# Softcap attention and a bilinear FFN on one core: load order, PSUM banks, row buffers and the start addresses of tiles

## The chip, the cores and the metric

The kernel runs on one core of one Trainium2 chip. The metric is device time in microseconds. A core has five engines that run side by side and wait for one another by semaphores: TensorE (matmuls, PE in the profile), VectorE (DVE), ScalarE (ACT), GpSimd (POOL) and SyncE (SP, which here issues most DMAs). Each engine works off its own instructions in the order in which they were written.

## The reference

```python
def _attn_ref(q, k, v, cap):              # q, k, v: (4, 12, 448, 64) float32
    scores = np.matmul(q, k.transpose(0, 1, 3, 2)) / np.sqrt(q.shape[-1])
    scores = cap * np.tanh(scores / cap)
    scores = scores - np.max(scores, axis=-1, keepdims=True)
    attn = np.exp(scores)
    attn = attn / (np.sum(attn, axis=-1, keepdims=True) + 1e-09)
    return np.matmul(attn, v)

def _moe_ref(x, w_a, w_b, w_out):         # x: (1792, 768), w: float64, d_ff 1536
    return ((x @ w_a) * (x @ w_b) @ w_out).astype(np.float32)
```

x is the attention output with the heads side by side. The weights arrive as float64, two 32-bit words per value.

## The kernel before

**Attention.** 48 heads are taken two at a time: 24 pairs, `NPG` = 12 of them make a group, which is half of the tokens. For a pair, `load_k` loads q and k in four blocks of 32 columns each (56 KB, runs of 128 bytes), `load_v` loads v in four pieces, `turn` transposes q and k in 32x32 blocks on VectorE. `scores` multiplies them in four chunks of keys (c = 0, 1, 2 of 128 keys per head and c = 3 with the last 64 of both heads), each into a PSUM tile of two banks. `tanh` and `exp` run on ScalarE; the softmax needs no maximum, since the cap bounds the scores. `add_full` and `add_last` add the chunks up on VectorE, `sums` adds that over partitions with 28 small matmuls against the selector `sel`, and `attend` multiplies the exponentials with v into one PSUM bank, `pv`. `recip` inverts the sums, `store_rec` writes them to memory (`rd`), `load_den` reads them back as a row for 64 partitions each (`den`), `scale` multiplies pv with it.

The first group's matmuls are in fp32 (each is two instructions), and its x is split at once into a high and a low fp32r part (`split_x`: `xhi`, `xlo`). The second group's scores are in fp32r with three products of high and low parts; its x goes to memory and comes back later.

**FFN.** `hidden` makes 448 tokens by 128 columns of x @ w_a or x @ w_b in 18 fp32r matmuls of 448 columns, `project` makes 128 tokens by 384 columns of the output in 9 of 384 columns, each into one PSUM bank. `keep_a`, `gate` and `collect` empty the banks. A weight is loaded as float64 words (`load64`, 768 KB), converted in six steps (`conv`: two on ScalarE, three on VectorE, one on GpSimd) and split (`split_hi`, `split_lo`).

**Order.** The order on TensorE is written by hand in `chain`: for the first group the four score chunks of a pair, then attend and sums of the pair before; then FFN pieces of the first group between the attention of the second (`ffn(GAP / 2)` twice a pair), then the second group's FFN. A planner places everything else: each job has an engine, a duration, a lag and what it needs, gets a due time back from TensorE's order, and each engine takes the ready job with the earliest due time. The fourth `job` argument after the needs, `after`, is an earliest time in the plan. It only orders the plan; on the chip an instruction waits for its data and its buffers alone.

**Buffers.** A pool with a tag and `bufs` hands out that many buffers, and the first instruction on a buffer waits for the last reader of the tile that had it. [...] In the first group scores have three tiles of two banks (`sc_one`) and pv has two banks; later scores have two tiles, the FFN two and one (`ff_a`, `ff_b`), pv one. In SBUF the tiles stand one behind the other; the framework's constants end at a multiple of 128 bytes, `capt` and `bounded` take 64 bytes, then come `sel` (512 bytes a partition), `psum0`, `psum1`, `xhi`, `xlo`, `acc` and the rest, all multiples of 128.

Of the kernel before, what the change touches and what calls it, by code (L numbers as in the profile page):

```python
# [118 lines left out]
def kernel(  # L119
# [54 lines left out]
    ps = {}  # L174

    def psum_pool(name, bufs, instead=None):
        if instead is not None:
            ps.pop(instead).close()
        ps[name] = fast.enter_context(ExitStack())
        side = "right" if name[:2] == "pv" or name == "ff_b" else "left"  # L180
        pool = tc.tile_pool(name=name, bufs=bufs, side=side, space=bass.MemoryType.PSUM, reuse_waits="tile")
        return ps[name].enter_context(pool)

    room = {"pv": psum_pool("pv_one", 2), "sc": psum_pool("sc_one", 3)}
# [4 lines left out]
    sel = const.tile([P, SUB, Q], F32, tag="sel", name="sel")  # L189
# [8 lines left out]
    raw, stk, prob, pvs = {}, {}, {}, {}  # L198

# [12 lines left out]
    def load_v(pi, n):  # L212
# [3 lines left out]
        eng = nc.gpsimd if 2 <= pi < NPG else nc.sync  # L216
# [30 lines left out]
    def scores(pi, c):  # L247
        tk, tq = stk["k", pi], stk["q", pi]
        psc = room["sc"].tile([P, 2, 512], F32, tag="pssc", name=f"psc_{pi}_{c}")
# [16 lines left out]
    def tanh(pi, c):  # L266
        hf, i = divmod(c, 2)
        if i == 0:
# [21 lines left out]
    def attend(pi, hf):  # L290
        if hf == 0:
            pvs[pi] = room["pv"].tile([P, 512], F32, tag="pv", name=f"pv_{pi}")
# [6 lines left out]
    def sums(pi):  # L299
        t = pvs[pi]  # L300
        for m in range(SUB):
            for i in range(P // Q):
# [6 lines left out]
                nc.tensor.matmul(to, sel[:, m], psum[pi % 2][:, j, c * SC : (c + 1) * SC], start=(m == 0), stop=last)  # L309

    def recip(pi):
        rec = sm.tile([P, SC], F32, tag="rec", name=f"rec_{pi}", bufs=1)
# [12 lines left out]
    xs, hold = {}, {}  # L325

# [97 lines left out]
    FB0 = 6  # L424

    def bank(name):
        n = len(took)
        took.append(name)
        if n == 0:
            room["sc"] = psum_pool("sc_two", 2, "sc_one")  # L430
            room["ff", 0] = psum_pool("ff_a", 2)
        elif n == FB0:
            room["pv"] = psum_pool("pv_two", 1, "pv_one")
            room["ff", 1] = psum_pool("ff_b", 1)
        late = n >= FB0 and (n - FB0) % 3 == 0
        return room["ff", int(late)].tile([P, 512], F32, tag="ff", name=name)

    took = []

# [58 lines left out]
    class Piece:  # L498
        def __init__(self, eng, us, lag, needs, fn, args, after):
            self.eng, self.us, self.lag, self.needs, self.fn, self.args, self.after = eng, us, lag, needs, fn, args, after  # L500
            self.due, self.then, self.order_only = 1e9, [], False
# [7 lines left out]
    def loads(pi, after=0.0):  # L509
        for nm in "kq":  # L510
            eng = "ACT" if nm == "q" and pi == 0 else "SP"
            for n in range(P // BLK):
                needs = [("load", nm, pi, n - 1)] if n else [("turn", nm, pi - 2)]
                job(("load", nm, pi, n), eng, 0.52, load_k, (pi, nm, n), needs, 2.4, after)
                jobs["load", nm, pi, n].order_only = n > 0
        for n in range(4):
            eng, us = ("POOL", 0.6) if 2 <= pi < NPG else ("SP", 0.52)
# [4 lines left out]
    def softmax(pi):  # L522
        for c in range(SUB):
            needs = [("tanh", pi, c - 2)] if c > 1 else []
            if c % 2 == 0:
                needs += [("attend", pi - 2, c // 2), ("add", pi - 2, c // 2)]
            if c == 2:
# [8 lines left out]
        job(("recip", pi), "DVE", 0.5, recip, (pi,), [("sums", pi), ("rd", pi - 1)])  # L536
        job(("rd", pi), "SP", 0.5, store_rec, (pi,), [("recip", pi)])
        free = [("x", pi - 2)]
        for j in range(2):
            job(("den", pi, j), "SP", 0.52, load_den, (pi, j), [("rd", pi), *([("den", pi, 0)] if j else free)])  # L540
# [18 lines left out]
    chain = []  # L559
# [5 lines left out]
    def scores_of(pi, c):  # L565
        ready = [("lo", nm, pi) for nm in "kq"] + ([("z", pi)] if c == NC3 else []) if pi >= NPG else [("turn", nm, pi) for nm in "kq"]
        back = 3 if pi < NPG else 2
        n = SUB * pi + c - back
        if (NPG - 1) * SUB < n < NPG * SUB and pi >= NPG:
            n = NPG * SUB - 1  # L570
# [266 lines left out]
```

## Time and profile before

| | us |
|---|---|
| median of 3 runs (739.11 to 1163.57) | 741.04 |
| profiled execution | 739.0 |
| its span, first to last instruction | 737.1 |
| TensorE busy | 711.3 (96%) |
| VectorE, ScalarE, GpSimd busy | 438.6, 347.7, 107.1 |
| granted TensorE clock, mean | 0.988 |

The busy time of TensorE counts pipelined matmuls whose ends are modelled, so 96% doesn't say that it runs at its peak. How fast matmuls follow one another is read from their start times in the timeline. The slowest of the three runs is far off the other two; the profile is of an execution beside these.

### The profile page before, as it was taken

The numbers are of one execution on the slowest core, as the hardware profiler recorded it, in microseconds if no ns is written. First come the engines' busy times: TensorE is split into PE (matmuls) and PEld (weight loads), VectorE is DVE, ScalarE is ACT, GpSimd is POOL, SyncE is SP. The second block draws the span as 40 slices with busy tenths as digits, with TensorE's granted clock in tenths as the row PEclk, the third lists the DMA queues.
The fourth block names the chain that finished last, engine by engine and source line by source line (L and its number), as shares of the span: only waits on it lengthen the run. The fifth ranks groups of instructions, "written<-read, shape, count | busy, mean of one in ns | idle before, by whom it ended". The sixth has DMA issues, their size and how long they took to land.

```text
span 737.1 us, 10930 instructions
## 1 busy us (share of the span) xinstructions
PE 711.3 (96%) x4242; PEld 578.7 (79%) x4242; DVE 438.6 (60%) x657; ACT 347.7 (47%) x474; POOL 107.1 (15%) x86
## 2 busy tenths in 40 slices
PE   5987999999999999999999999999999999999996
PEld 2333337788887798778788779999999999999996
DVE  3588988968766877885986747442033434334222
ACT  3888785676875864675757630122321112202100
POOL 2224242222212312312222100000000000000000
PEclk8899999999999999999999999999999999999999
DMA  9679675656866665656355427322022103101012
GB/s 163 121 130 161 129 165 149 163 177 167 211 194 167 172 175 162 185 167 179 117 178 154 141 82 256 108 86 64 1 86 65 43 22 108 44 21 44 1 44 110
DMA packets 141914, 90.53 MB, mean 123 GB/s; under 512 B 107104, under 2 KB 127648, under 8 KB 141856
## 3 DMA queue, kind: packets, MB, share of 16 engines
q1 hardware_dynamic: 137152, 82.53, 42.4%
q0 software_dynamic: 2848, 7.02, 3.6%
q8 instruction: 35, 0.57, 0.3%
q10 hardware_dynamic: 1856, 0.23, 0.3%
q14 instruction: 23, 0.19, 0.1%
HBM read 67.24 MB, written 22.50 MB: 122 GB/s over the span
## 4 chain that ended last, share of the span: by engine, by line
PE 83%; DMA 7%; SPq 3%; DVE 3%; ACT 2%; issue 1%; POOL 0%; ACTq 0%; DVEq 0%; POOLq 0%
PE phb L445 8%; PE phb L447 8%; PE phb L446 8%; PE pha L445 8%; PE pha L446 8%; PE pha L447 8%; PE po L478 8%; PE po L480 7%; PE po L479 7%; PE pv L297 7%; PE psc L260 3%; DMA den<-rd 3%; SPq L210 2%; DMA rd<-rec 2%; PE psc L255 2%; PE psc L263 1%
## 5 line engine op out<-in xcount | busy, mean ns | idle before, releaser
L478 PE MATMUL po<-who,gh 128*128 128x384 f32 x336 | 113.4, 338 | 1.9 <-DVE acc L489 1.5
L480 PE MATMUL po<-who,gl 128*128 128x384 f32 x336 | 112.4, 334 | 0.0
L479 PE MATMUL po<-wlo,gh 128*128 128x384 f32 x336 | 112.3, 334 | 0.0
L445 PE MATMUL pha<-xhi,wha 128*128 128x448 f32 x288 | 106.1, 369 | 0.8 <-DVE xhi L345 0.8
L445 PE MATMUL phb<-xhi,whb 128*128 128x448 f32 x288 | 106.1, 369 | 0.0
L446 PE MATMUL pha<-xlo,wha 128*128 128x448 f32 x288 | 105.8, 367 | 0.2 <-DVE xlo L346 0.2
L447 PE MATMUL pha<-xhi,wla 128*128 128x448 f32 x288 | 105.7, 367 | 0.0
L447 PE MATMUL phb<-xhi,wlb 128*128 128x448 f32 x288 | 105.6, 367 | 0.0
L446 PE MATMUL phb<-xlo,whb 128*128 128x448 f32 x288 | 105.6, 367 | 0.0
L272 ACT ACTIVATE pf<-psc,capt 128x896 f32<-128x896 f32 x96 | 82.7, 912 | 35.3 <-PE psc L260 20.0
L297 PE MATMUL pv<-pf,vb 128*64 128x448 f32 x384 | 79.2, 555 | 6.4 <-DVE den L329 6.4
L276 ACT ACTIVATE pf<-pf,capt 128x1792 f32<-128x1792 f32 (+1 forms) x48 | 77.2, 1611 | 0.5
L489 DVE TENSOR_TENSOR acc<-po,acc 128x384 f32<-128x384 f32 x84 | 46.2, 554 | 41.5 <-PE po L480 41.4
L452 ACT COPY asb<-pha 128x448 f32<-128x448 f32 x48 | 25.6, 533 | 93.3 <-PE pha L447 91.3
L464 ACT CAST gh<-asb 128x448 fp32r<-128x448 f32 x48 | 27.2, 567 | 88.5 <-DVE asb L462 88.1
L297 PEld LDWEIGHTS pv<-pf,vb 128*64 128x64 f32 x384 | 25.8, 138 | 53.1 <-issue 39.2
L478 PEld LDWEIGHTS po<-who,gh 128*128 128x128 f32 x336 | 63.0, 188 | 4.8 <-DVE acc L489 2.7
L462 DVE TENSOR_TENSOR asb<-phb,asb 128x448 f32<-128x448 f32 x48 | 29.9, 622 | 59.7 <-PE phb L447 59.6
L479 PEld LDWEIGHTS po<-wlo,gh 128*128 128x128 f32 x336 | 63.1, 188 | 0.2
L480 PEld LDWEIGHTS po<-who,gl 128*128 128x128 f32 x336 | 63.1, 188 | 0.0
L445 PEld LDWEIGHTS pha<-xhi,wha 128*128 128x128 f32 x288 | 54.1, 188 | 6.9 <-DVE xhi L345 1.2
L445 PEld LDWEIGHTS phb<-xhi,whb 128*128 128x128 f32 x288 | 54.1, 188 | 6.3 <-issue 1.2
(94 smaller groups left out, 1049.2 us busy)
## 6 DMA issues: line engine op xcount, KB each, us to landing
w64o<-in_moe_w_out_dram SPq DMA_DIRECT2D x12, 768.0 KB
w64a<-in_moe_w_a_dram SPq DMA_DIRECT2D x9, 768.0 KB
w64b<-in_moe_w_b_dram SPq DMA_DIRECT2D x9, 768.0 KB
ldk<-in_k_dram SPq DMA_DIRECT2D x96, 56.0 KB
den<-rd SPq DMA_DIRECT2D x48, 112.0 KB
ldq<-in_q_dram SPq DMA_DIRECT2D x92, 56.0 KB
out_dram<-acc SPq DMA_DIRECT2D x13, 384.0 KB
wda<-wta SPq DMA_DIRECT2D x12, 384.0 KB
```

The costliest lines, as they stand in the source:

```text
L272: nc.scalar.activation(to, prob.pop((pi, "s", c))[:, :n, :S], AF.Tanh, scale=capt[:, 1:2])
L276: nc.scalar.activation(pf, pf, AF.Exp, scale=capt[:, 0:1])
L297: nc.tensor.matmul(t[o, :S], tv[:, j * (NC3 + 1) + (c if j == 0 else (c + 1) % (NC3 + 1))], p, start=(c == 0), stop=(c == NC3))
L445: nc.tensor.matmul(t[:, :S], wh[:, kk], xhi[:, kk, cs], start=(kk == 0), stop=False)
L446: nc.tensor.matmul(t[:, :S], wh[:, kk], xlo[:, kk, cs], start=False, stop=False)
L447: nc.tensor.matmul(t[:, :S], wl[:, kk], xhi[:, kk, cs], start=False, stop=(kk == NK - 1))
L462: nc.vector.tensor_mul(t, phs.pop(("b", h))[:, :S], t)
L464: nc.scalar.copy(gs[g, f][0][:, cs], t)
L478: nc.tensor.matmul(t[:, :HALF], gh[:, cs], wh, start=(f == fs[0]), stop=False)
L479: nc.tensor.matmul(t[:, :HALF], gh[:, cs], wl, start=False, stop=False)
L480: nc.tensor.matmul(t[:, :HALF], gl[:, cs], wh, start=False, stop=(f == fs[-1]))
L489: nc.vector.tensor_add(acc[:, ti, hs], t, acc[:, ti, hs])
```

## The change

- Loads: v of pair 2 is loaded from SP and not from GpSimd; `cap` is loaded from ScalarE's queue behind q of pair 0; the planned earliest time of the weight loads goes from 12.0 to 18.0 (`RAW`); longer lags are planned for the first loads, for `rd` and for `den`. The warm-up is five matmuls (ten instructions) and comes ahead of the other memsets.
- PSUM: two score tiles throughout, and one pool of four single banks for pv and the FFN.
- Order on TensorE: in the first group chunks 0 and 1, attend of the pair before, chunks 3 and 2, sums of two pairs before. `GAP` 20.4; 3.6 us of FFN pieces around pair 12. A piece of `hidden` may be planned before its later x rows are there (`early`).
- The selector is a block of ones in a tile of 56 columns, from which a window is taken.
- `rec` has two buffers; `den` of pairs 10 and 11 is lent from the FFN's gate buffers.
- Addresses: `sel` moves to the end, a tile of 64 bytes, `even`, stands in its place.

```diff
-    room = {"pv": psum_pool("pv_one", 2), "sc": psum_pool("sc_one", 3)}
+    ps_sc = fast.enter_context(tc.tile_pool(name="ps_sc", bufs=2, space=bass.MemoryType.PSUM))
+    ps_1 = fast.enter_context(tc.tile_pool(name="ps_1", bufs=4, space=bass.MemoryType.PSUM))
+
+    def bank(name):
+        return ps_1.tile([P, 512], F32, tag="ps1", name=name)
...
-    sel = const.tile([P, SUB, Q], F32, tag="sel", name="sel")
+    const.tile([P, 16], F32, tag="even", name="even")
...
+    ends = fast.enter_context(tc.tile_pool(name="ends", bufs=1))
+    sel = ends.tile([P, 2 * Q - QS], F32, tag="sel", name="sel")
...
-        eng = nc.gpsimd if 2 <= pi < NPG else nc.sync
+        eng = nc.gpsimd if 3 <= pi < NPG else nc.sync
...
-                nc.tensor.matmul(to, sel[:, m], psum[pi % 2][:, j, c * SC : (c + 1) * SC], start=(m == 0), stop=last)
+                nc.tensor.matmul(to, sel[:, Q - (m + 1) * QS : 2 * Q - (m + 1) * QS], psum[pi % 2][:, j, c * SC : (c + 1) * SC], start=(m == 0), stop=last)
...
-            pvs[pi] = (pvs[pi][0], sm.tile([P, S], F32, tag="den", name=f"den_{pi}"))
+            if pi in LENT:
+                den = f32(gp.tile([P, GT], F32R, tag=LENT[pi], name=f"den_{pi}", bufs=GF)[:, :S])
+            else:
+                den = sm.tile([P, S], F32, tag="den", name=f"den_{pi}")
+            pvs[pi] = (pvs[pi][0], den)
...
+    LENT = {NPG - 2: "gh", NPG - 1: "gl"}
...
-                job(("load", nm, pi, n), eng, 0.52, load_k, (pi, nm, n), needs, 2.4, after)
+                job(("load", nm, pi, n), eng, 0.52, load_k, (pi, nm, n), needs, 3.2 if pi < 2 else 2.4, after)
...
-            on_pe(("attend", pi, hf), 1.52, attend, (pi, hf), [("exp", pi, hf), free, *(("load", "v", pi, n) for n in range(4))])
+            on_pe(("attend", pi, hf), 1.52, attend, (pi, hf), [("exp", pi, hf), *banks[-4:-3], *(("load", "v", pi, n) for n in range(4))])
+        banks.append(("scale", pi))
...
-    WARM, SOON = 3, 4.0
-    GAP = 19.4
+    WARM, SOON, RAW = 5, 4.0, 18.0
+    GAP = 20.4
...
-        for c in range(SUB):
+        for c in (0, 1):
             scores_of(pi, c)
         if pi:
             attend_of(pi - 1)
+        for c in (3, 2):
+            scores_of(pi, c)
+        if pi > 1:
+            sums_of(pi - 2)
...
-            job(("raw", t), "POOL" if t < 6 else "SP", 0.6, load64, (t,), [("conv", t - 2, 5)], 6.0, 12.0)
+            job(("raw", t), "POOL" if t < 6 else "SP", 0.6, load64, (t,), [("conv", t - 2, 5)], 6.0, RAW)
...
+        warm = bank("warm")
+        nc.vector.memset(psum[0][:, 0], 0.0)
+        for _ in range(WARM):
+            nc.tensor.matmul(warm[:, :S], psum[0][:, 0, :P], psum[0][:, 0], start=True, stop=True)
...
+    def load_cap():
+        nc.scalar.dma_start(capt[:, 3:4], cap.rearrange("(a b) -> a b", b=1).to_broadcast([P, 1]))
+
+    job("cap", "ACT", 0.5, load_cap, (), [("load", "q", 0, 3)], 2.4)
```

## Rows read from the trace of the kernel before

**Rows 1.** The page, busy time, its share of the span, and instructions.

```profile
PE 711.3 (96%) x4242; PEld 578.7 (79%) x4242; DVE 438.6 (60%) x657; ACT 347.7 (47%) x474; POOL 107.1 (15%) x86
```

**Rows 2.** Timeline, stretch 0 to 110: start us, length, engine, line, out<-in [idle <-releaser].

```profile
2.75 4.48 PE L710 MATMUL warm<-psum 128*128 128x448 f32 x6 [2.75 <-DVE psum L708]
...
3.97 0.86 POOL L365 DMA_DIRECT2D w64a<-in_moe_w_a_dram  x1
...
8.08 0.65 DVE L226 STREAM_TRANSPOSE tq<-ldq 128x448 f32<-128x448 f32 x1 [4.91 <-DMA ldq<-in_q_dram]
...
9.31 5.07 PE L255 MATMUL psc<-tq,tk 64*128 64x448 f32 x16 [2.08 <-DVE capt L718]
...
18.05 6.20 PE L255 MATMUL psc<-tq,tk 64*128 64x448 f32 x16 [3.68 <-DVE tq L226]
...
27.62 0.89 ACT L375 ACTIVATE w64a<-w64a 128x768 int32<-128x768 uint32 x1
...
27.92 3.43 PE L255 MATMUL psc<-tq,tk 64*128 64x448 f32 x16
...
109.71 0.47 PE L445 MATMUL pha<-xhi,wha 128*128 128x448 f32 x1
```

**Rows 3.** Busy time by stage: stretch, length, engines, granted clock, DMA share, GB/s.

```profile
27.90:59.70 31.80, 28.17 (x222) 10.79 (x216) 24.54 (x39) 28.38 (x28) 10.12 (x16) 1.00 0.76 127
59.70:79.50 19.80, 16.57 (x148) 6.48 (x149) 17.29 (x26) 14.94 (x15) 9.16 (x12) 0.91 0.85 169
79.50:109.70 30.20, 28.49 (x246) 11.27 (x240) 28.10 (x42) 27.13 (x27) 10.97 (x14) 1.00 0.71 149
```

**Rows 4.** Waits from 27.9 to 109.7: engine line <- releaser: us, times, longest.

```profile
PE pv L297 <- DVE den L329: 6.4, 4, 2.4
...
PE pv L309 <- DVE psum L283: 1.8, 2, 1.0
```

**Rows 5.** Groups of instructions by shape: busy us, mean ns | idle before.

```profile
L478 PE MATMUL po<-who,gh 128*128 128x384 f32 x336 | 113.4, 338 | 1.9 <-DVE acc L489 1.5 <-DVE asb L462 0.3
...
L445 PE MATMUL pha<-xhi,wha 128*128 128x448 f32 x288 | 106.1, 369 | 0.8 <-DVE xhi L345 0.8
...
L272 ACT ACTIVATE pf<-psc,capt 128x896 f32<-128x896 f32 x72 | 68.9, 1005 | 35.3 <-PE psc L260 20.0 <-PE psc L255 14.7 <-DVE rec L313 0.6
...
L479 PEld LDWEIGHTS po<-wlo,gh 128*128 128x128 f32 x336 | 63.1, 188 | 0.2
...
L309 PEld LDWEIGHTS pv<-psum,sel 128*32 128x32 f32 x672 | 11.7, 109 | 19.7 <-DVE psum L283 6.8 <-DVE gl L467 2.1 <-issue 2.1
```

**Rows 6.** Timeline of TensorE: first and last of 55 hidden, of 94 projection matmuls.

```profile
480.04 0.37 PE L445 MATMUL pha<-xhi,wha 128*128 128x448 f32 x1
...
491.20 0.37 PE L445 MATMUL phb<-xhi,whb 128*128 128x448 f32 x1
...
515.01 0.33 PE L478 MATMUL po<-who,gh 128*128 128x384 f32 x1
...
531.13 0.33 PE L478 MATMUL po<-who,gh 128*128 128x384 f32 x1
```

**Rows 7.** Timeline, weight loads of fp32 attend: first and last of six steps.

```profile
24.61 0.14 PEld L297 LDWEIGHTS pv<-pf,vb 128*64 128x64 f32 x2 [0.23 <-issue]
...
26.49 0.14 PEld L297 LDWEIGHTS pv<-pf,vb 128*64 128x64 f32 x2 [0.23 <-issue]
```

**Rows 8.** DMA issues by line and engine: KB each, median us from issue to landing.

```profile
w64a<-in_moe_w_a_dram POOLq DMA_DIRECT2D x3, 768.0 KB, 6.3
```

**Rows 9.** Chain that ended last, in order of time: start us, us, what.

```profile
14.89 2.42 DMA vb<-in_v_dram
...
147.73 1.43 PE psc L260 x12
```

**Rows 10.** Timeline of VectorE behind the last attend: reciprocal and scale.

```profile
441.65 0.56 DVE L313 RECIPROCAL rec<-pv 112x64 f32<-112x64 f32 x1 [1.60 <-PE pv L309]
...
451.71 0.62 DVE L329 TENSOR_TENSOR den<-pv,den 128x448 f32<-128x448 f32 x1 [1.74 <-DMA den<-rd]
```

More of the change, by code (lines that the diff above doesn't have):

```diff
@@ L422 @@
     phs, asb, gs = {}, {}, {}
[L424 to L438, printed above, removed]
     def hidden(g, f, nm, h):
@@ L523, in softmax @@
         for c in range(SUB):
[L524 to L527, printed above, removed]
+            needs = [("attend", pi - 2, c // 2), ("add", pi - 2, c // 2)]
+            if c > 1:
                 needs += [("add", pi - 2, "l")]
@@ L535, in softmax @@
         g, r = divmod(pi, NPG)
-        job(("recip", pi), "DVE", 0.5, recip, (pi,), [("sums", pi), ("rd", pi - 1)])
-        job(("rd", pi), "SP", 0.5, store_rec, (pi,), [("recip", pi)])
-        free = [("x", pi - 2)]
+        job(("recip", pi), "DVE", 0.5, recip, (pi,), [("sums", pi), ("rd", pi - 2)])
+        job(("rd", pi), "SP", 0.7, store_rec, (pi,), [("recip", pi)], 3.0)
+        own_den = [p for p in range(pi) if p not in LENT]
+        free = [("x", own_den[-2])] if pi not in LENT and len(own_den) > 1 else []
         for j in range(2):
-            job(("den", pi, j), "SP", 0.52, load_den, (pi, j), [("rd", pi), *([("den", pi, 0)] if j else free)])
+            job(("den", pi, j), "SP", 0.52, load_den, (pi, j), [("rd", pi), *([("den", pi, 0)] if j else free)], 3.0)
             jobs["den", pi, j].order_only = j > 0
@@ L593, in ffn_piece @@
             on_pe(key, 3.6, hidden, (g, f, x, h), needs)
+            kind = "xl" if g else "x"
+            jobs[key].early = {id(jobs[kind, h * NP + kk]): 0.6 * kk for kk in range(NP) if (kind, h * NP + kk) in jobs}
             if x == "a":
@@ L659 @@
                 scores_of(pi, c)
-            ffn(GAP / 2)
-            for c in range(2, SUB):
+            ffn(GAP / 2 if pi > NPG else 3.6)
+            for c in (3, 2):
                 scores_of(pi, c)
-            ffn(GAP / 2)
+            ffn(GAP / 2 if pi > NPG else 3.6)
     ffn(1e9)
@@ L702, in warm_up @@
     def warm_up():
[L703 to L710 removed]
+        warm = bank("warm")
+        nc.vector.memset(psum[0][:, 0], 0.0)
+        for _ in range(WARM):
+            nc.tensor.matmul(warm[:, :S], psum[0][:, 0, :P], psum[0][:, 0], start=True, stop=True)
+        for t in vb:
+            for j in range(2):
+                nc.vector.memset(t[own[1 - j], NC3 + j], 0.0)
         nc.vector.memset(sel, 0.0)
@@ L713, in warm_up @@
             nc.vector.memset(f32(z), 0.0)
-        for m in range(SUB):
-            nc.vector.memset(sel[:, m, m * QS : (m + 1) * QS], 1.0)
+        nc.vector.memset(sel[:, Q - QS : Q], 1.0)
     def limits():
@@ L786 @@
             y.left -= 1
-            y.ready = max(y.ready, t + x.us if y.order_only and y.eng == x.eng else x.end)
+            y.ready = max(y.ready, t + x.us if y.order_only and y.eng == x.eng else x.end - y.early.get(id(x), 0.0))
             if not y.left and y.eng != "PE":
@@ L794 @@
             x.fn(*x.args)
-    for pool in reversed(ps.values()):
-        pool.close()
     fast.close()
```

58 lines of the change are left out of this document (18 added, 40 removed).

## Prediction

> **What bounds the kernel now.** I read the page first: TensorE is busy in 96% of the span [rows 1], so a gain can only come from the few places where it waits, or from its matmuls following one another faster. The profiled execution took 739.0 us, 1.9 more than its span of 737.1, and the median of the runs shown is 741.0; I sum against 739.0.
>
> For the waits I read the timeline of the start. Scores begin at 9.31 for the first pair, 18.05 for the second and 27.92 for the third [rows 2]. The cause stands beside it: the first transpose waits 4.91 us for the last block of q, while a weight load of 768 KB, issued by GpSimd at 3.97 (a second one follows it), moves on the same DMA engines [rows 2]. Next I read the busy time by stage, from the third pair to the first FFN matmul at 109.71: TensorE is busy 28.17 + 16.57 + 28.49 = 73.2 of 81.8 us, ScalarE 70.5, VectorE 69.9 [rows 2, 3]. Three engines are near their limit, none at it. (The granted clock of the middle stage is 0.91: part of it ran at the lower level, 1.2 GHz; that stays in the 73.2.) The list of waits for that stretch tells where TensorE's 8.6 idle us go: 6.4 to attend waiting for the scale of two pairs back (store of the reciprocals, load of the rows, product), 1.8 to sums waiting for the adds [rows 4]. From 109.7 on TensorE hardly waits, apart from 0.8 us for xhi [rows 5].
>
> So the rest of the time is the pace of the FFN matmuls, and here the timeline shows something odd. Projection matmuls (384 columns) follow one another in (531.13 - 515.01) / 93 = 173.3 ns, hidden ones (448 columns) in (491.20 - 480.04) / 54 = 206.7 ns [rows 6]. At 2.4 GHz that is 416 and 496 columns, 32 and 48 more than they stream. It isn't a fixed cost of every matmul: the fp32 attend steps come each (26.49 - 24.61) / 5 = 376 ns for 448 columns passed twice, 373.3 + 2.7 [rows 7]. Nor is it the time of a weight load: 32 columns take 109 ns and 128 take 188 [rows 5], so 0.82 ns a column, 105 ns for 128, well under 160.
>
> **The change part by part.**
>
> *Alignment.* The two tiles ahead of `sel` take 64 bytes and all later sizes are multiples of 128, so before the change every operand starts 64 bytes past a multiple of 128; `even` in place of `sel` puts it on the multiple. If a moving operand is fetched in lines of 128 bytes (32 columns), 384 columns from the middle of a line touch 13 of them, and 13 x 32 = 416 is to the column what the row shows. 448 columns touch 15, 480 columns, and the row shows 16 more [rows 6]. Aligned, one line goes: 13.3 ns a matmul. There are 6 x 288 hidden and 3 x 336 projection matmuls [rows 5]: 2736 x 13.3 ns = 36.5 us. Bounds: nothing, if the excess has nothing to do with addresses; and all of it above the 2.7 ns that fp32 shows, 17.3 x 1728 + 10.6 x 1008 ns = 41 us. I take 36.5, because 13 lines fit without a remainder and because fp32, where a column has two clocks and an extra line has time to arrive, shows no such cost at the same offset.
>
> [...]
>
> *First loads.* The v loads of pair 2 leave GpSimd's queue, and the weight loads are planned from 18.0 on instead of 12.0. By the planner's own durations k and q of pair 0 are there at 4 x 0.52 + 3.2 = 5.3, its first tanh starts at 7.8, its second exp ends at 14.4 and its attend at about 17.3. That is below 18.0, so the v loads of pair 3 come first in GpSimd's queue; they wait for that attend to free their buffer, and the weight loads are queued behind this wait. What is late next is the conversion of the weights. It began at 27.62 [rows 2]; issued near 20, with 6.3 us to land [rows 8], the first weights come near 27, and TensorE needs them near 100: nothing. The 448 KB of the first q and k then have the DMA engines alone. cap goes behind q on ScalarE's queue, where only the table load and the first tanh are behind it, and leaves SP's head, 0.4 us. Ten warm-up instructions instead of six, 0.75 us each [rows 2], end at 7.5 to 8.8, about when the first scores can start; they hide under the loads. SP then issues 8 blocks for pair 1 at some 0.5 us (the planner's figure), 2.42 us to land [rows 9], 1.25 for two transposes: scores near 13. v of pairs 0 and 1 and q, k of pair 2 are 16 more issues: third scores near 20.5 instead of 27.92. v of pair 2 puts four issues, 2.1 us, on SP; the loads of pair 3 behind them have a pair's time of 7 us to spare.
>
> *Order of the fp32 phase, banks, selector, lent rows.* Sums move one pair later and attend gets four banks, so a scale has two more attends' time before anyone waits: the 6.4 and 1.8 us go. Against it, scores keep two buffers instead of three, and attend stands between chunks 0, 1 and 3, 2, so a chunk's tanh has to end while TensorE does other work. The trace has no such order. Bounds: nothing (two tanh take 2 us [rows 5], attend over 3), and one tanh of 1.0 us for each of ten pairs, 10 us. ScalarE and VectorE are busy 70 of the 73 us, so they follow with little slack, and I take 5.3 us. First FFN matmul: 20.5 + 73.2 + 5.3 = 99.0 against 109.7, 10.7 us gained, with ends of 1 and 18 (loads and waits both at their worst or best). The selector has as many matmuls of the same size: nothing. A second `rec` and two lent rows only take away waits of SP and VectorE that TensorE doesn't see: nothing.
>
> *FFN phase.* GAP and the new order move pieces between pairs; their number stays. The first pieces may start before all x are split: the 0.8 us goes. pv now shares four banks with the FFN instead of having its own; if the pool hands on the bank that was freed first, the FFN keeps three in turn, as before: nothing.
>
> Sum: 739.0 - 36.5 - 10.7 - 0.8 = 691.0 us.
>
> **Rivals.**
>
> *Addresses don't matter*; the excess belongs to one-pass matmuls, or to a weight swap that fp32's double pass hides. For it: every operand stands at the same offset, so no row compares two. Against it: the fit to 416. Then 739.0 - 11.5 = 727.5. [...] No run shows a second offset yet.
>
> *pv's bank stalls the FFN.* If banks go round strictly, the fourth piece behind an attend waits for its scale. From the reciprocal to the end of the scale it took 452.3 - 441.7 = 10.7 us [rows 10]; two score chunks and three projections take 1.43 [rows 9] + 3 x 1.56 = 6.1. In the new order four projections follow the attends of pairs 14, 17 and 20, and that of pair 23 without scores: 3 x 4.6 + 6.0 = 20 us, 711. Three hidden pieces take 11 us and hide it.
>
> *Aligned starts cost.* The 16 columns that the line count leaves over at 448 [rows 6] say that something else, such as how the weight stream and the moving stream meet, matters too; both starting on a line's edge could meet worse. From 11.5 us / 2736 = 4.2 ns more per matmul the kernel is slower than before; a line more, 13.3 ns, gives 764. Against it: nothing in a row makes an aligned start the worse one.
>
> **How the numbers follow.** Forecast, 691: 0.52. Addresses don't matter, 727: 0.27. Bank stalls, 711: 0.10. Aligned starts cost, 764: 0.06. Something else: 0.05. The forecast's own range is 676 to 702, from the ends of its terms. Up to 732 the range takes in 711 and most of 727, and leaves out some 0.15. Within 2% is about what a measurement tells from no change: 726 to 756. Faster takes the forecast, the bank stalls and 0.10 of the 727 case, 0.72; same the rest of that case and a little more, 0.19; slower 0.09.
>
> **What would show it.** In the new profile projections follow in 160 to 163 ns and hidden matmuls in 187 to 194; at 173 and 203 to 207 that step is wrong and 727 is left. GpSimd's first weight load starts after 17 us, the third scores near 20.5, the first FFN matmul near 99, and no attend waits for den before that. Bank stalls would show as waits of `po` for den behind pairs 14, 17, 20 and 23. The phase order is wrong if TensorE's waits for tanh in the fp32 phase grow by more than 10 us.

## The result, and the profile after

Before 740.03 us, after 744.18 us (medians); the ratio is 1.0059, 95% interval 1.0041 to 1.0078. That is 0.6% slower: a loss that the measurement can tell from nothing, and too small to count as slower at 2%. The forecast was 691 with a range of 676 to 732; the time is above its upper end. The profiled execution took 743.4 us, its span 741.5.

TensorE is as busy as before, 96% of the span [rows 1]. This is the page of the changed kernel (busy us, share, instructions):

```profile
PE 713.1 (96%) x4246; PEld 577.8 (78%) x4246; DVE 431.7 (58%) x654; ACT 347.9 (47%) x474; POOL 102.7 (14%) x82
```

The pace of the matmuls, for which 36.5 us were forecast, hasn't moved. Timeline of TensorE in the changed kernel, the first and last of 55 hidden and of 94 projection matmuls, to be held against [rows 6]:

```profile
484.39 0.37 PE L430 MATMUL pha<-xhi,wha 128*128 128x448 f32 x1
...
495.55 0.37 PE L430 MATMUL phb<-xhi,whb 128*128 128x448 f32 x1
...
514.68 0.34 PE L463 MATMUL po<-who,gh 128*128 128x384 f32 x1
...
530.80 0.33 PE L463 MATMUL po<-who,gh 128*128 128x384 f32 x1
```

(495.55 - 484.39) / 54 = 206.7 ns and (530.80 - 514.68) / 93 = 173.3 ns, the same to the tenth as before.

The start did move. Timeline of the changed kernel (start us, length, engine, line, out<-in):

```profile
5.25 0.65 DVE L222 STREAM_TRANSPOSE tq<-ldq 128x448 f32<-128x448 f32 x1 [2.54 <-DMA capt<-in_cap_dram]
...
7.32 1.77 PE L251 MATMUL psc<-tq,tk 64*128 64x448 f32 x8
...
17.70 2.73 PE L251 MATMUL psc<-tq,tk 64*64 64x448 f32 x12
...
20.02 0.86 POOL L366 DMA_DIRECT2D w64a<-in_moe_w_a_dram  x1
...
105.78 0.47 PE L430 MATMUL pha<-xhi,wha 128*128 128x448 f32 x1
```

The first transpose comes at 5.25 us where it came at 8.08, and the first weight load leaves GpSimd at 20.02 where it left at 3.97 [rows 2]. The row at 17.70 holds the last two chunks of the second pair and the first of the third, whose first instruction starts at 19.45 in the trace, against 27.92. Part of this is TensorE's clock. Before, the granted clock was 0.50 from 18.0 to 23.0 us, and the second pair's scores, from 18.05 on, took 6.20 us where the third's took 3.43 [rows 2]; after the change it is 1.00 over the whole start. Busy time and granted clock (0.82, then 1.00) of the start, before and after:

```profile
0.00:27.90 27.90, 19.39 (x82) 7.50 (x82) 10.57 (x32) 14.62 (x15) 5.56 (x12) 0.82 0.82 144
```

```profile
0.00:19.40 19.40, 16.33 (x58) 5.99 (x59) 9.56 (x29) 12.23 (x12) 2.29 (x7) 1.00 0.63 108
```

But the first FFN matmul comes at 105.78, only 3.9 us earlier than 109.71. The busy time by stage, to be held against [rows 3] (stretch, length, PE, PEld, DVE, ACT, POOL, granted clock, DMA share, GB/s):

```profile
19.40:50.00 30.60, 28.22 (x210) 9.78 (x208) 20.77 (x28) 27.52 (x28) 13.98 (x20) 1.00 0.78 169
50.00:80.00 30.00, 24.50 (x216) 8.71 (x212) 24.89 (x41) 22.84 (x22) 10.77 (x15) 1.00 0.66 145
80.00:105.80 25.80, 24.40 (x209) 8.91 (x209) 23.76 (x35) 23.95 (x25) 6.92 (x9) 0.93 0.78 194
```

TensorE is busy 77.1 of 86.4 us here, and was 73.2 of 81.8; the new order has the sums of one more pair in this stretch, 0.65 us. The waits of that stretch, to be held against [rows 4] (us in total, times, longest):

```profile
PE psc L251 <- ACT pf L268: 4.6, 5, 2.7
PE pv L293 <- ACT pf L272: 2.9, 2, 1.6
PE pv L293 <- DVE den L330: 1.7, 1, 1.7
```

Attend's wait for the scale of an earlier pair has gone from 6.4 to 1.7 and that of sums for the adds is gone, as forecast; waits for tanh and exp, 7.5 us, stand in their place.

By stage, worked out from these starts and the two spans:

| | before | after | difference |
|---|---|---|---|
| start to the third pair's scores | 27.9 | 19.45 | -8.5 |
| from there to the first FFN matmul | 81.8 | 86.3 | +4.5 |
| from there to the end | 627.4 | 635.7 | +8.3 |

Summed over TensorE's timeline, each piece to the start of the next, the 8.3 us are 3.8 at the 112 projections (183.3 for 179.5), 3.4 at attend and sums of pair 12, 1.1 in the rest. The projections stop at two of the places that the second rival had named. These are waits of TensorE behind 105.8 us, the projections' for scales, and at pair 12 the sums' for the adds and attend's for its exp:

```profile
PE po L463 <- DVE den L330: 4.1, 2, 2.5
PE pv L305 <- DVE psum L279: 2.1, 1, 2.1
...
PE pv L293 <- ACT pf L272: 1.0, 1, 1.0
```

The scale that the first of the two projections waits for, in VectorE's timeline, waits itself for its rows of reciprocals from memory:

```profile
283.72 0.63 DVE L330 TENSOR_TENSOR den<-pv,den 128x448 f32<-128x448 f32 x1 [2.75 <-DMA den<-rd]
```

Behind that stop the granted clock is 0.50 from 285.5 to 288.5. Busy time and granted clock (0.68) from 284.0 to 287.6:

```profile
284.00:287.60 3.60, 3.11 (x12) 3.06 (x12) 3.57 (x8) 0.00 (x0) 0.00 (x0) 0.68 0.59 144
```

So two stretches lost what the start had gained, and the largest term of the sum was nothing. The runs below ask why, part by part.

### The profile page after: what moved, and what is told of

It reads as the page before. It is cut to its first block, busy times and chain, and to the rows that moved or that the text cites. A ratio compares the mean times of both kernels' runs of the same rounds, so it can differ in the third digit from the quotient of the medians.

```text
span 741.5 us, 10936 instructions
## 1 busy us (share of the span) xinstructions
PE 713.1 (96%) x4246; PEld 577.8 (78%) x4246; DVE 431.7 (58%) x654; ACT 347.9 (47%) x474; POOL 102.7 (14%) x82
## 3 DMA queue, kind: packets, MB, share of 16 engines
q1 hardware_dynamic: 137968, 82.76, 40.1%
## 4 chain that ended last, share of the span: by engine, by line
PE 83%; DVE 7%; DMA 4%; SPq 3%; ACT 2%; issue 1%; POOL 0%; DVEq 0%; POOLq 0%
PE phb L430 8%; PE pha L430 8%; PE phb L432 8%; PE phb L431 8%; PE pha L432 8%; PE pha L431 8%; PE po L463 7%; PE po L464 7%; PE po L465 7%; PE pv L293 6%; PE psc L256 3%; DMA den<-rd 3%; PE psc L251 1%; SPq L206 1%; PE pv L305 1%
## 5 line engine op out<-in xcount | busy, mean ns | idle before, releaser
L268 ACT ACTIVATE pf<-psc,capt 128x896 f32<-128x896 f32 (+1 forms) x96 | 84.2, 910 | 47.0 <-PE psc L256 31.9
L432 PE MATMUL pha<-xhi,wla 128*128 128x448 f32 x288 | 105.8, 368 | 0.0
L431 PE MATMUL pha<-xlo,wha 128*128 128x448 f32 x288 | 105.8, 367 | 0.0
L431 PE MATMUL phb<-xlo,whb 128*128 128x448 f32 x288 | 105.8, 367 | 0.0
L272 ACT ACTIVATE pf<-pf,capt 128x1792 f32<-128x1792 f32 (+1 forms) x48 | 77.1, 1607 | 0.7
```

The source lines that it names most:

```text
L272: nc.scalar.activation(pf, pf, AF.Exp, scale=capt[:, 0:1])
L431: nc.tensor.matmul(t[:, :S], wh[:, kk], xlo[:, kk, cs], start=False, stop=False)
L432: nc.tensor.matmul(t[:, :S], wl[:, kk], xhi[:, kk, cs], start=False, stop=(kk == NK - 1))
```

## Experiments

The parts were put on one at a time, in both directions. A is the aligned starts (with the sliding selector), L the first loads, O the rest (order, PSUM, GAP, row buffers). Ratios are to the kernel before, run beside each kernel. The kernels ran on different chips, so where two of them are compared, the difference of their medians and that of their ratios are both given.

| kernel | A | L | O | us | ratio, 95% interval |
|---|---|---|---|---|---|
| before | | | | 740 to 742 | 1 |
| a1_align | A | | | 734.7 | 0.9896, 0.9867 to 0.9925 |
| e2_queued | A | L | | 739.1 | 0.9991, 0.9971 to 1.0010 |
| c1_order | A | | O | 751.8 | 1.0117, 1.0089 to 1.0146 |
| n1_noalign | | L | O | 749.9 | 1.0132, 1.0100 to 1.0163 |
| after | A | L | O | 744.2 | 1.0059, 1.0041 to 1.0078 |

### Aligned starts: a1_align, n1_noalign, m1_pace

a1_align puts the pad and the sliding selector into the kernel before, n1_noalign takes the pad out of the changed kernel:

```diff
-    sel = const.tile([P, SUB, Q], F32, tag="sel", name="sel")
+    const.tile([P, 16], F32, tag="even", name="even")
...
```

> The kernel before with one part of the change: the pad of 64 bytes in place of the selector, and the sliding selector at the end, so that xhi, xlo and the weights begin at multiples of 128 bytes. Nothing else differs. If a moving operand is fetched in lines of 128 bytes: projections 160 ns and hidden matmuls 190 ns apart, 739 - 36.5 = 702 us. If addresses don't matter: 173 and 203 to 207 ns as in [rows 6], 739 to 741 us, a ratio within 0.003 of 1.

Neither came: the matmuls keep 173 and 203 to 207 ns, and yet the kernel is 1.0% faster, 734.7 us. n1_noalign shows it from the other side:

> The changed kernel without the pad: every tile begins 64 bytes past a multiple of 128 again, everything else as changed. If the aligned starts quicken the DMA traffic (a1_align: 735 for 741): 749 to 753 us, the first transpose later than 5.25 us, hardware queue at 42% of the DMA engines' span where the changed kernel has 40.1, matmuls 173 and 203 to 207 ns apart in both. If a1_align's gain was the shorter selector or the planner's order: 743 to 745 us.

749.9 us, 0.7% above the changed kernel, with the same pace of matmuls. So the aligned starts are worth 5 to 8 us in either kernel, and not by the pace of matmuls. The page's line of DMA queues has it (packets, MB, share of 16 engines' span), first the kernel before, then a1_align, with the same packets and bytes:

```profile
q1 hardware_dynamic: 137152, 82.53, 42.4%
```

```profile
q1 hardware_dynamic: 137152, 82.53, 40.9%
```

(n1_noalign 41.5%, after 40.1%.) In the packet records of the traces the 86,016 packets of 128 bytes, which are the blocks of q and k, take 14.2 ns on average before and 12.6 in a1_align, 13.5 in n1_noalign and 12.6 after. It isn't a price that each packet pays: the median is 13 ns in all four. What goes is a tail, the packets over 13 ns: 7,740 before and 497 in a1_align, 5,910 in n1_noalign and 544 after. In a1_align's timeline the first transpose then starts 1.55 us earlier than in [rows 2], its loads issued in the same order:

```profile
6.53 0.65 DVE L228 STREAM_TRANSPOSE tq<-ldq 128x448 f32<-128x448 f32 x1 [3.48 <-DMA ldk<-in_k_dram]
```

Its third pair's scores start at 23.86 us for 27.92 before, and from there to the first FFN matmul it takes 81.7 us for 81.8: in this execution the gain is made in the start. In n1_noalign's it looks otherwise: against the changed kernel TensorE's idle time is the same (28 us), and its busy time is 7.3 us longer at a lower granted clock (720.4 us at 0.983, 713.1 at 0.994). That the pad acts through the loads is shown by the packets; how late loads turn into these us is not taken apart.

What the pad moves for these packets is the address that they are written to; no run here separates the tiles.

m1_pace asks for the pace itself, with 16 series of 60 matmuls put ahead of the changed kernel's work, such as

```python
for i in range(60):
    nc.tensor.matmul(warm[:128, :448], xlo[:, i % 3, 0:128], xhi[:, i % 6, 16:464], start=True, stop=True)
```

> The changed kernel with 16 series of 60 matmuls ahead of its work, all operands zero, each series changing one thing: 448 columns accumulated as hidden does; single; moving operand 64, 16 and 4 bytes off; weights 64 bytes off; 384 columns, and 64 bytes off; 256; 512; weights of 64 columns with 448 and 384; two banks in turn; bf16 448 and 384; 448 again. The time of the whole says nothing (some 170 us more). If a start off the 128 bytes costs a line of 32 columns: 13 ns more in the series that are off. If addresses don't matter: 203 to 207 ns for 448 at each start, 173 for 384. If the excess belongs to the weight load of 128 columns: 189 and 162 ns with 64. If it belongs to the 4-byte type: bf16 at 189 and 162.

Timeline of TensorE in m1_pace, from the second series on; a series runs back to back with the next, so that (next start - start) / 60 is the spacing:

```profile
27.57 12.32 PE L701 MATMUL warm<-xhi,xlo 128*128 128x448 f32 x60
39.73 12.17 PE L703 MATMUL warm<-xhi,xlo 128*128 128x448 f32 x60
51.74 12.16 PE L705 MATMUL warm<-xhi,xlo 128*128 128x448 f32 x60
63.74 12.56 PE L707 MATMUL warm<-xhi,xlo 128*128 128x448 f32 x60
76.14 12.30 PE L709 MATMUL warm<-xhi,xlo 128*128 128x448 f32 x60
88.27 10.57 PE L711 MATMUL warm<-xhi,xlo 128*128 128x384 f32 x60
98.68 10.56 PE L713 MATMUL warm<-xhi,xlo 128*128 128x384 f32 x60
109.07 7.36 PE L715 MATMUL warm<-xhi,xlo 128*128 128x256 f32 x60
116.26 13.79 PE L717 MATMUL warm<-xhi,xlo 128*128 128x512 f32 x60
129.89 12.30 PE L719 MATMUL warm<-xhi,xlo 128*64 128x448 f32 x60
142.03 10.56 PE L721 MATMUL warm<-xhi,xlo 128*64 128x384 f32 x60
152.43 12.33 PE L723 MATMUL warm<-xhi,xlo 128*128 128x448 f32 x60
164.59 11.53 PE L725 MATMUL warm<-xhi,xlo 128*128 128x448 bf16 x60
175.96 9.91 PE L727 MATMUL warm<-xhi,xlo 128*128 128x384 bf16 x60
185.57 12.45 PE L729 MATMUL warm<-xhi,xlo 128*128 128x448 f32 x60
```

All operands are zero. In this order: 448 columns 202.7 ns; moving operand 64 bytes off 200.2, 16 bytes 200.0, 4 bytes 206.7; weights 64 bytes off 202.2; 384 columns 173.5, 64 bytes off 173.2; 256 columns 119.8; 512 columns 227.2; 64 weight columns with 448 and 384: 202.3, 173.3; two banks in turn 202.7; bf16 448 and 384: 189.5, 160.2. A start 64 or 16 bytes off costs nothing, one 4 bytes off 4.0 ns (one series). Weights of 64 columns load faster (134 ns for 188), and the spacing is the same. Between 256 and 512 columns lie 107.3 ns, so a column takes 0.42 ns. What lies above the columns by that is 14.8, 12.5, 12.5 and 12.5 ns at 448, 384, 256 and 512 columns of 4 bytes, nearly the same at each size, and 1.7 and -0.8 ns in bf16. The forecast's lines of 32 columns would have given 256 columns, eight whole lines, no excess. It is a price of some 12 to 15 ns for each matmul of the 4-byte type. That the type alone makes the difference isn't separated: the bf16 series also keep the same weights and columns throughout, and their weight loads take 98 ns. Nor does it give all of the 206.7 ns of [rows 6], which is 18.9 above the columns.

Of the expected 189 and 162 ns (within a ns of the columns with the 2.7 ns of [rows 7] above them, 189.4 and 162.7, an estimate) bf16 came to 189.5 and 160.2; 64 weight columns of the 4-byte type came to 202.3 and 173.3.

### First loads: b1_loads, e1_both, e2_queued, c1_order

> The kernel before with the first loads alone: v of pair 2 on SP, weight loads planned from 18.0 on, cap behind q on ScalarE's queue, five warm-up instructions; order, banks, selector and addresses as before. Theory A (the gain of the loads is real, and the new order and the shared banks gave it back): third pair's scores near 19.4 as after the change, 8.5 us earlier than [rows 2], first FFN matmul near 101, about 731 us, ratio 0.988. Theory B (the fp32 phase is set by ScalarE and VectorE, busy 70 of 82 us in [rows 3], so that an earlier start is lost again whatever the order): third scores near 19.4 too, first FFN matmul at 106 or later, 737 to 740 us.

750.9 us, ratio 1.0116 (1.0089 to 1.0143), and the reason is none of the theories. Of the weight load the edit moves only the time in the plan, and the planned 18.0 held nothing back on the chip: it left at 1.27. In the old order attend of pair 0 is planned later, so the planner put the weight load ahead of the v loads of pair 3, first in GpSimd's queue. Timeline of b1_loads:

```profile
1.27 0.97 POOL L365 DMA_DIRECT2D w64a<-in_moe_w_a_dram  x1 [0.81 <-POOLq L823]
...
10.53 0.65 DVE L226 STREAM_TRANSPOSE tq<-ldq 128x448 f32<-128x448 f32 x1 [7.70 <-DMA ldq<-in_q_dram]
```

The load leaves at 1.27 and the first transpose waits until 10.53. In the changed kernel the loads come late (20.02) only because they are queued behind v loads that wait for an attend. e1_both has the aligned starts and the first loads, and was to mend this with a dependency on these v loads for the first weight (against b1_loads):

```diff
...
-load64, (t,), [("conv", t - 2, 5)], 6.0, RAW)
+load64, (t,), [("conv", t - 2, 5), *([("load", "v", 3, 3)] if t == 0 else [])], 6.0, RAW)
```

> The kernel before with two parts of the change: the aligned starts (pad and sliding selector, as in a1_align) and the first loads, with the first weight load queued behind the v loads of pair 3 as it is in the changed kernel (in b1_loads it had come to the head of GpSimd's queue, at 1.27 us). Order of the fp32 phase, banks, rows and GAP as before. Theory C (three parts that add: aligned starts -7.7 us by the DMA traffic, as a1_align; first loads -7.6, c1_order less the changed kernel; new order and banks +18, c1_order less a1_align): 734.7 - 7.6 = 727 us, first FFN matmul near 98. Rival (the fp32 phase takes what ScalarE and VectorE need, an earlier start is lost): 733 to 736 us, first FFN matmul at 104 to 106.

The second weight then went first, again at 1.27 us; 736.8 us, 0.9937 (0.9910 to 0.9964). e2_queued holds both (`t < 2`):

> The kernel before with aligned starts and the first loads, both weight loads now queued behind the v loads of pair 3 (in e1_both one of them had still gone first, at 1.27 us, and the first scores began at 10.27). Order and banks as before. If the gain of an earlier start lasts in the old order: first scores near 7.3, first FFN matmul near 100, 728 to 730 us. If the old order's own waits take it back (attend for den 6.7, sums for psum 2.6 in a1_align; ScalarE busy 75 us of 86): 733 to 736 us, first FFN matmul at 104 or later.

739.1 us. First scores at 7.96, attend of pair 0 at 15.94 where a1_align has 19.90, and the first FFN matmul at 105.58 where a1_align has 105.60. Four us of head start are gone before the FFN, and the whole is not faster than a1_align but 0.6% (by the medians) to 1.0% (by the ratios) slower. Some 3 us of it go in one place, attend of pair 2, first in e2_queued, then in a1_align:

```profile
34.79 6.20 PE L299 MATMUL pv<-pf,vb 128*64 128x448 f32 x16 [3.27 <-DVE den L331]
```

```profile
36.36 3.23 PE L299 MATMUL pv<-pf,vb 128*64 128x448 f32 x16 [1.98 <-DVE den L331]
```

It waits 3.27 us for the scale of pair 0, and then runs 6.20 us instead of 3.23: the granted clock from 34.8 to 41.0 is 0.51. The next scores begin at 41.50, where a1_align has 41.26. (Later it leads again by 2.2 us, at 55.68 for 57.87, and loses this too, at further waits for scales and adds.)

c1_order does the reverse, the changed kernel with the old loads:

```diff
-    WARM, SOON, RAW = 5, 4.0, 18.0
+    WARM, SOON, RAW = 3, 4.0, 12.0
-        eng = nc.gpsimd if 3 <= pi < NPG else nc.sync
+        eng = nc.gpsimd if 2 <= pi < NPG else nc.sync
...
```

> The changed kernel with the first loads put back as before (v of pair 2 on GpSimd, weight loads from 12.0, cap on SP, three warm-up instructions); order, banks, selector, lent rows and addresses as changed. Theory A: third scores near 28, first FFN matmul near 28 + 86 = 114, about 752 us, 1.016 of before. Theory B (the fp32 phase takes what ScalarE and VectorE need): the late start is caught up, first FFN matmul 106 to 110, 744 us or less.

751.8 us, as theory A had it in total; but not in place: its first FFN matmul comes at 107.98 and most of the loss lies behind it, where its projections take 188.8 us and TensorE waits 8.2 us (4.1 after) for scales. With the new order the first loads are worth 0.6% (ratios) to 1.0% (medians), with the old one less than nothing.

### The new order in the fp32 phase: e1i_inter, o1_inarow, o2_inarow

e1i_inter gives e1_both the interleaved chunks, with sums still right behind attend:

```diff
...
-        for c in range(SUB):
+        for c in (0, 1):
             scores_of(pi, c)
         if pi:
             attend_of(pi - 1)
+        for c in (3, 2):
+            scores_of(pi, c)
...
```

> e1_both with one part of the new order: attend of the pair before stands between score chunks 0, 1 and 3, 2. Three score buffers, two pv banks of their own and sums right behind attend stay as before. If the interleaving itself costs (a chunk's tanh doesn't end in time, TensorE changes between kinds of work once more per pair, some 0.3 us): 5 to 10 us above e1_both. If it only costs with two score buffers: within 2 us of e1_both.

766.5 us, 1.0347 (1.0312 to 1.0383), far beyond both. TensorE's waits up to its first FFN matmul at 133.68:

```profile
PE pv L311 <- DVE psum L285: 25.4, 11, 6.2
```

With attend earlier, sums right behind it meet adds that aren't done. That the change also moves sums a pair later is what makes its interleaving possible. The other way round, the changed kernel with the chunks in a row:

> The changed kernel with the four score chunks of a pair in a row (0, 1, 2, 3) and attend behind them, in the fp32 phase; two score buffers, shared banks, sums of two pairs back, loads and addresses as changed. If the interleaving is what costs 18 us: 735 us or less. If two buffers are what costs (a chunk waits for the tanh of the chunk two back, 1.0 us, and for the exp before it): 748 us or more. If it is what is queued in the shared banks: 742 to 746.

748.5 us, but here too the weight loads had gone to the head of the queue. o2_inarow holds them:

> The changed kernel with the four score chunks of a pair in a row in the fp32 phase, as o1_inarow, with the weight loads held behind the v loads of pair 3 (in o1_inarow they had gone to the head of GpSimd's queue and the first scores began at 12.0, not 7.32). If the interleaving is what costs: 738 us or less. If two score buffers are what costs: 748 us or more, with more waits for tanh. If neither (the loss lies behind the fp32 phase, in the shared banks): 742 to 746 us.

749.3 us, 1.0112 (1.0077 to 1.0147). TensorE's waits up to the first FFN matmul at 111.3:

```profile
PE psc L251 <- ACT pf L268: 14.0, 14, 3.4
```

14.0 us where the changed kernel has 6.3 in the same stretch: with two score buffers the interleaving gains, and it isn't the loss. What the two buffers cost by themselves isn't shown, since no run gives the changed kernel a third.

### Shared banks: d1_ownbank, d2_ownbank

Both keep one of the four single banks for pv, in the fp32 phase of some pairs and from pair 12 on of all. The edit of d2_ownbank:

```diff
+    OWN = {f"pv_{i}" for i in (3, 7, *range(NPG, NPAIR))} | {"pha_0_0_0"}
...
+        if name in OWN:
+            return ps_v.tile([P, 512], F32, tag="psv", name=name)
```

> The changed kernel, with a bank that only pv uses (every fourth pair of the fp32 phase, each pair from 12 on) and three banks for the rest, so that no projection stands behind a scale. Theory A (shared banks cost what the trace after shows at 280 and 452: 2.7 + 0.8 + 0.8 us of TensorE at the lower clock behind it + 1.7 + 1.8, of which the drain had 1.2 before): 744.2 - 6 = 738 us, no wait of po for den. Rival (the wait only moves: attend waits for its bank instead, or fewer banks make the FFN wait for its own reads): 743 to 746 us.

744.4 us, 1.0035 (1.0018 to 1.0052): the projections' stalls went (178.3 us), but the first FFN piece waited 4.5 us for a scale, and the fp32 phase was 7 us longer. d2_ownbank keeps the turn of the banks up to there:

> The changed kernel with one bank kept for pv of pairs 12 to 23 (in the fp32 phase for pairs 3 and 7 and for the first FFN piece, so that the turn of the four banks up to there stays as it was); d1_ownbank had made the first FFN piece wait 4.5 us for a scale. If shared banks cost the projections' stalls: po doesn't wait for den, 179 us for 112 projections where the changed kernel has 183, 738 to 740 us. If the wait only moves: 743 to 746 us.

741.3 us, 0.9999 (0.9978 to 1.0020), between the two answers. The projections take 177.8 us and none waits for den, 5.5 us less than after; but there is a new wait (TensorE, behind 107 us):

```profile
PE phb L436 <- DVE den L336: 3.6, 1, 3.6
```

The shared banks cost the changed kernel 3 (medians) to 4 us (ratios) net. Wherever a bank is taken from, the next user waits for a scale.

### What takes the head start: t1_lags to t4_lags, x1_noconv, x2_norows

In the changed kernel two transfers came later than planned, and each stood in a queue that keeps its order. Timelines of TensorE, VectorE and ScalarE:

```profile
55.50 1.72 PE L293 MATMUL pv<-pf,vb 128*64 128x448 f32 x8 [1.67 <-DVE den L330]
...
58.47 1.73 PE L293 MATMUL pv<-pf,vb 128*64 128x448 f32 x8 [1.25 <-ACT pf L272]
...
54.82 0.62 DVE L330 TENSOR_TENSOR den<-pv,den 128x448 f32<-128x448 f32 x1 [5.20 <-DMA den<-rd]
...
56.18 0.93 ACT L376 ACTIVATE w64a<-w64a 128x768 int32<-128x768 uint32 x1 [3.43 <-DMA w64a<-in_moe_w_a_dram]
...
57.01 1.41 ACT L272 ACTIVATE pf<-pf,capt 128x1344 f32<-128x1344 f32 x1
```

VectorE waits 5.2 us for the rows of den, and with it the scale that attend at 55.50 needs; ScalarE waits 3.4 us for the weight, and with it the exp behind it that attend's second half at 58.47 needs. t1_lags tells the planner longer times, so that these waits stand later:

```diff
...
-store_rec, (pi,), [("recip", pi)], 3.0)
+store_rec, (pi,), [("recip", pi)], 3.5)
...
-*([("den", pi, 0)] if j else free)], 3.0)
+*([("den", pi, 0)] if j else free)], 5.0)
...
-6.0, RAW)
+9.5, RAW)
```

> The changed kernel with three numbers of the planner: 9.5 us instead of 6.0 from a weight load's issue to its landing, 5.0 instead of 3.0 for a row load of den, 3.5 instead of 3.0 for the store of the reciprocals, so that conversions and scales stand later in the queues of ScalarE and VectorE. If transfers later than planned are what takes the start's gain (a conversion waits with an exp behind it): ScalarE's 3.6 us for w64a and VectorE's 8.5 us for den in the fp32 phase go, first FFN matmul near 98, 737 us. If not: 743 to 746 us, first FFN matmul 104 to 107, waits elsewhere.

742.8 us, 1.0008 (0.9989 to 1.0027): a gain of 0.2 (medians) to 0.5% (ratios), and the first FFN matmul stays at 105.55. ScalarE's wait for w64a is gone and others have come, of TensorE and of ScalarE in that stretch:

```profile
PE pv L293 <- DVE den L330: 5.4, 4, 2.5
...
PE pv L305 <- DVE psum L279: 3.1, 1, 3.1
...
PE psc L251 <- ACT pf L268: 0.5, 2, 0.3
...
ACT wha L410 <- POOL wta L390: 6.2, 2, 4.8
```

The same numbers in three other kernels:

> d2_ownbank (the changed kernel with a bank for pv) with the same three numbers. If both causes add: 741.3 - 7 = 734 us. If the numbers do nothing: 740 to 742 us.

743.8 us, 1.0018 (1.0002 to 1.0034): nothing gained.

> a1_align (before with aligned starts) with the same three numbers (9.5 for 6.0; 5.0 and 3.5 for 2.4). If late transfers in ordered queues are the cause: below 732 us. If the old order's wait of attend for the scale of two pairs back sets it: 733 to 737 us, or more where the scale, put later, comes later.

> e2_queued (before with aligned starts and first loads) with the same three numbers. If late transfers are what takes the first loads' gain: 731 us or less, first FFN matmul below 100. If the old order's wait for the scale: 737 to 740 us.

752.3 us, 1.0126 (1.0099 to 1.0153), and 750.6 us, 1.0111 (1.0082 to 1.0140). With two pv banks a scale that is placed later makes attend wait 14.5 and 18.0 us for den (6.7 in a1_align, 7.6 in e2_queued). It is the wait at which e2_queued loses its head start above: there the old order doesn't run ahead of its scales.

The last two take away one suspect each.

> The changed kernel, but of the first six weights' conversion only one ScalarE operation of six is left (0.8 us; left out: 0.82 us of ScalarE, 1.84 of VectorE and 2.1 of GpSimd for each weight, so these weights are not the reference's). If the fp32 phase is set by the work of ScalarE and VectorE, 74 and 69 us busy of 86: first FFN matmul near 97, 735 us. If by the scale's way through memory or by loads of q and k: 103 to 106, 741 us or more.

```diff
+        if t < 6:
+            wt = wp.tile([P, DM], I32, tag="wt", name=f"wt{nm}_{f}", bufs=AHEAD)
+            nc.scalar.activation(f32(wt), f32(wraw[t][:, :, 1]), AF.Abs)
...
```

749.1 us, 1.0106 (1.0059 to 1.0152): with less work for ScalarE, VectorE and GpSimd it is slower, the first FFN matmul at 113.16. With the conversions shortened the later weight loads come sooner (the third leaves GpSimd at 29.32 us, 48.09 after): the DMA share of the stretch is 0.83 (0.73 after), and the transfers land late. ScalarE's wait for a weight, and VectorE's for rows (8.5 after):

```profile
ACT w64o L382 <- DMA w64o<-in_moe_w_out_dram: 10.0, 2, 8.4
...
DVE den L330 <- DMA den<-rd: 18.0, 6, 4.2
```

> The changed kernel without the store of the reciprocals and the row loads of den (left out: the division by the sums; a scale multiplies by one, right behind the reciprocal). If the scale's way through memory sets the fp32 phase (attend and the x of the FFN wait for it, VectorE stands behind it): first FFN matmul near 97 and no stall of a projection later, 730 us. If ScalarE and VectorE's own work sets it: first FFN matmul 102 to 105; the projections' stalls go all the same, 737 us.

```diff
...
-        nc.vector.tensor_mul(den, t[:, :S], den)
+        nc.vector.tensor_scalar_mul(den, t[:, :S], rec[:, 0:1])
...
```

723.7 us, 0.9770 (0.9738 to 0.9802). (By the edit the scale multiplies by the first column of the reciprocals in 112 partitions, and by one only in the other 16; the work is the same.) The first FFN matmul comes at 97.85, and the 112 projections take 176.3 us. Busy time from 19.4 to there:

```profile
19.40:97.85 78.45, 74.49 (x631) 27.12 (x627) 69.34 (x115) 72.85 (x72) 32.55 (x41) 1.00 0.70 152
```

ScalarE and VectorE do the same work as after (72.9 and 69.3 us, 74.3 and 69.4 there) in 78.4 us instead of 86.4. So neither engine's work sets the length of the fp32 phase: it is the way of the reciprocals through memory. Of the 19.5 us between its span and the changed kernel's 7.9 lie there and 11.6 behind it. The run takes away both the wait and the traffic of 48 row loads of 112 KB; it doesn't say how much each is worth.

## Why the prediction was wrong

The profiled execution took 743.4 us, 52.4 more than 691.0. Of these 36.5 are the alignment, 6.8 the way to the first FFN matmul (105.8 for 99.0), and 9.1 the stretch behind it, which apart from the alignment became 8.3 us longer where 0.8 less was forecast.

- **Alignment, -36.5 us: wrong, the term that failed.** The step was that 416 columns are 13 lines of 32. It rested on one size and one start address, and a fixed 13 ns for each matmul fits 384 columns just as well. Measured, matmuls that start at a multiple of 128 bytes follow one another in 173.3 and 206.7 ns as before, and m1_pace has no gain for them over a start 64 bytes off; it has a price of 12 to 15 ns for each matmul of the 4-byte type, at 256 columns as at 512. The 2.4 GHz by which the forecast counts columns is 0.417 ns for each, and m1_pace has 0.419 (107.3 ns for 256 columns). The forecast had written the 16 columns left over at 448 down to "something else"; they were the sign. It had ruled out a fixed price by the fp32 attend (2.7 ns above its two passes), which showed only that fp32 doesn't pay it. The rival *Addresses don't matter* had the mechanism right on TensorE. What nobody had in the list is that DMAs mind the start: 5 to 8 us, from a1_align and n1_noalign.
- **First loads: the number right to the third pair's scores** (20.5 forecast, 19.45 came), and right that the first weight load would stand behind v of pair 3. In part it was luck: the 20.5 were summed from issues and loads, but the third pair's transposes end at 16.79, and its scores wait for TensorE's and ScalarE's own work. And some 2.8 of the 8.5 us (6.20 less 3.43 for the second pair's scores) are a clock that the forecast had no term for. (The lower level, 1.2 GHz, that it names for the middle stage is a granted clock of 0.50 from 75.0 to 78.0 us of before, where the attend steps at 76.24, 76.99 and 77.74 come 0.75 us apart, against the 376 ns of [rows 7].)
- **Phase order, first FFN matmul at 99.0: wrong, 105.8.** The waits for den and the adds fell about as forecast (8.2 to 1.7 us). The exchange was put at 5.3 us of remaining waits; TensorE's idle time in the stretch was 9.3, and its busy time 77.1 instead of 73.2. Of these 3.9 us 2.6 are gone in x2_norows (74.5 busy, granted clock 1.00 there, 0.93 in the last stage after), so they belong to the waits; 0.65 are the sums of one more pair. The failing thought was that four banks let a scale be late at no price. A late row also stops VectorE, and the adds, transposes and scales behind it; a late weight stops ScalarE and the exp behind it.
- **Tanh waits** grew by less than the 10 us named as the sign of a wrong order; the sign was badly chosen, since exp and scale share the loss.
- **Bank stalls: the rival's mechanism came, at half its places.** Projections stood still behind the attends of pairs 17 and 23, for 2.7 and 3.4 us (where before had 1.2 behind pair 23); those of pairs 14 and 20 didn't. 20 us were forecast for this case, and the projections lost 3.8. d2_ownbank shows what the banks are worth, 3 to 4 us.
- **xhi wait, -0.8:** it went, but attend of pair 12 waits 1.0 us for its exp instead, and its sums 2.1 us for adds, which stand on VectorE behind a scale that waits 1.7 us for its rows.
- **Aligned starts cost:** didn't come; they gain.
- **The range** ended at 732, since it let the alignment fail but kept 11.5 us from the start. (Its inner range, 676 to 702, isn't quite what the ends of its terms give, 679 to 701.) No case had both terms fail, though each stood on an order of work that no row of before showed.

Still open: how the extra time of O without L (c1_order against a1_align, 17 us) divides among GAP, row buffers and the planner's new placing, why L costs 0.6 to 1.0% in the old order though its first FFN matmul comes at the same time, and why hidden matmuls take 206.7 ns in [rows 6] and 202.7 in m1_pace. a1_align, before with aligned starts alone, has the lowest time of a whole kernel, 734.7 us; that of e1_both, 736.8, can't be told from it (their intervals overlap).

## What to carry to other kernels

A pattern that fits one size without a remainder is no measurement: before a large term is put on it, look for a second size or type that it must get wrong. Ahead of a change that starts work earlier, find the loop that the work must go round (here attend, sums, store, row load, scale), because the head start is lost there unless that loop gets shorter; taking the loop away is the experiment that shows it. And in queues that keep their order, ask of each wait on a DMA what stands behind it when the transfer is three us late.

## What the runs showed of the hardware

- A matmul of the 4-byte type follows another 12 to 15 ns later than its columns take at 0.42 ns each, at 256 to 512 columns, with starts 64 or 16 bytes off too (19 ns with a start 4 bytes off, and in the hidden matmuls of [rows 6]); bf16 within 2 ns of its columns (m1_pace).
- Blocks of 128-byte runs load faster where the tiles begin at multiples of 128 bytes: 12.6 ns a packet for 14.2 on average, by a tail of slow packets that goes (9.0% of them over 13 ns, then 0.6%), and 0.7 to 1.0% of this kernel's time (before against a1_align, n1_noalign against after).
- One weight load of 768 KB at the head of a queue moves the first transpose from 5.41 us (e2_queued) to 9.04 (e1_both, the same kernel but for the place of that load).
- A wait of TensorE can cost more than its length: behind 3.27 us of waiting in e2_queued attend ran at a granted clock of 0.51 and took 6.20 us, where a1_align's took 3.23.
